# Banded attention and two feed-forward layers on one core: four weight pieces' joins one step later, the second load of v ahead of keys and queries

## The chip, the cores and the metric

One core of a Trainium2 chip runs the whole program. The time is device microseconds of one execution, the median of several. A core has five engines that run their own queues in order and meet at semaphores: TensorE (PE in the profile; its weight loads PEld), VectorE (DVE), ScalarE (ACT), GpSimd (POOL) and SyncE (SP), which issues all the DMA transfers of this kernel. The granted clock of TensorE has two levels, 1.2 GHz (0.5) and 2.4 GHz (1.0).

## The reference

Attention with a local band and block summaries, then two feed-forward layers. Shapes: q, k, v are 2 x 8 x 768 x 64; the first layer is 512 to 2048 to 512, the second 512 to 1024 to 512, on 1536 tokens.

```
k_sum = k.reshape(B, H, nb, 32, D).max(axis=3)
v_sum = v.reshape(B, H, nb, 32, D).mean(axis=3)
scores_l = scale * q @ k.T          # only |i - j| < 16 counts, else -1e9
scores_s = scale * q @ k_sum.T + log(32)
a = softmax(concat(scores_l, scores_s))
x = a @ concat(v, v_sum)            # heads put side by side: 1536 x 512
h = x @ w_in;  x = (h * cos(h)) @ w_out
h = x @ w_in2; solu = h * softmax(h)
out = (layer_norm(solu) * g_ln) @ w_out2
```

The weights come as 64-bit floats.

## The kernel before, in words

The order of the instructions is written out by hand: each engine gets them in the order in which the program names them, and only waits stand between.

The attention takes two heads at a time (a pair n, 0 to 7) and cuts the 768 rows of a pair into 12 tiles of 64 rows; four tiles make a group, so there are three groups to a pair and 24 in all. The loop `for step in range(NGR + LA)` (L663) is a pipeline over groups: n, g = divmod(step, 3). In one step the scores of group step + 1 are made on TensorE (`emit_s`, sps, L561), the maximum of group step on VectorE (`emit_max`, L572) and its subtraction on GpSimd (L576), the exponential of group step - 1 on ScalarE (L581), the sum of step - 2 on VectorE (L585), its normalization on GpSimd (`emit_norm`, L591), the transposes of step - 4 on TensorE (`emit_t`, aps, L598), their copy on ScalarE (`emit_at`, L603), the product with v of step - 5 (`emit_av`, ops, L613) and its copy into X on ScalarE (`emit_x`, L627).

Keys and queries are loaded two pairs or more ahead. In steps with g = 1 (1, 4, 7, 10, 13, 16) VectorE puts the two heads of pair n + 2 side by side (`pair_k`, kg, and `pair_q`, qg, both L426). In the next step, g = 2, TensorE transposes them (`emit_k` L494, `emit_q` L533), and ScalarE copies the queries (`emit_qx` L547). In the step after that, g = 0, VectorE makes the maxima of the key blocks (`emit_ksum` L506) and ScalarE the windows of keys (`emit_kx` L515, `emit_kx_ends` L522, L525 in the next step). The scores of pair n + 2 then need kx.

v is loaded by `load_v` (four DMA issues, L440 and L444, of which two hold the ends); four buffers. `sum_v` (L472) makes its block sums on TensorE at the steps of VSUM_AT, `scale_v` (vm, L480) copies them, `place_vsum` (L487) puts them into v's tile by DMA one step later. The sums of pairs 0 to 6 use the bank that the first product of the feed-forward layer (h, L277) needs at step 19.

A weight piece is 128 x 512 words of 64 bits and goes through these stages, one a step: `bits` at a step of WSTEPS opens it and issues the load of the piece after it (L141, three buffers); in the next step `rebias` (two ScalarE activations, L162 and L163) and `finish` (the join on VectorE, L169); in the step after that `split` (a cast on ScalarE, L186, and a subtraction on GpSimd, L187). The first eight pieces belong to the first layer and go through during the attention. XS are the steps in which a part of X is split in the same way (L246, L247). From step 19 on `fill` puts products of the first layer (h, L277) between the attention's. Behind the attention come the first layer (h L277, y L319) and the second (h L911, L1078), in which the weights of later layers go through the same stages.

Of the kernel before, what the change touches and what calls it, by code (L numbers as in the profile page):

```python
# [34 lines left out]
def fused_kernel(  # L35
# [56 lines left out]

    wide = w_in.dtype == mybir.dt.int64
    LOWEST = -3.0e38
    WSTEPS = (6, 9, 12, 15, 17, 18, 20, 21)
    XS = (7, 10, 13, 16)
    IDLE = (0, 0, 0)
    DVE_X = 19
# [243 lines left out]
    def warm_up(n):  # L342

        if not n:
            return
        idle = idles[0]
        t = ps_h0.tile([P, 512], F32, tag="h", name="idle")
        for _ in range(n):
            nc.tensor.matmul(t, lhsT=idle[:, 0:P], rhs=idle, start=True, stop=True)
# [35 lines left out]
    def attention():  # L385
        st = ExitStack()
        with st:
# [41 lines left out]
            def pair_k(n):  # L429
                k_t[n] = side_by_side(k_t[n], "kg", nc.gpsimd if n == 1 else nc.vector)  # L430

            def pair_q(n):
                q_t[n] = side_by_side(q_t[n], "qg", (nc.gpsimd, nc.scalar)[n] if n < 2 else nc.vector)

            def load_v(n):
                b, hp = divmod(n, NP)
                t = io.tile([P, NT, 2, D], F32, tag="vt", name="vt", bufs=4)
                for j in range(2):
                    o = v[b, 2 * hp + j].offset
                    nc.sync.dma_start(  # L440
                        out=t[0:WIN, 1:NT - 1, j, :],
                        in_=bass.AP(v.tensor, o + (QT - BAND) * D, [[D, WIN], [QT * D, NT - 2], [1, D]]),
                    )
                    nc.sync.dma_start(  # L444
                        out=t[0:WIN, 0:NT:NT - 1, j, :],
                        in_=bass.AP(v.tensor, o, [[D, WIN], [(S - WIN) * D, 2], [1, D]]),
                    )
                v_t[n] = t
# [34 lines left out]
            def place_vsum(n):  # L483
                m = vs_t.pop(n)
                for c in range(2):
                    at = WIN + c * NS // 2
                    nc.sync.dma_start(  # L487
                        out=v_t[n][at:at + NS // 2].rearrange("p t j d -> p t (j d)"),
                        in_=m[D * c:D * c + NS // 2].unsqueeze(1).to_broadcast([NS // 2, NT, 2 * D]))
# [8 lines left out]
            def emit_k(n):  # L498
                qk = ps_qk.tile([P, 2, 2, S // 2], F32, tag="qk", name="qk")
                transposed(k_t.pop(n), qk[:, 0, 0], qk[:, 0, 1])  # L500
                qk_t["k", n] = qk[:, 0]
                qk_t["q", n] = qk[:, 1, 0], qk[:, 1, 1]
# [25 lines left out]
            def emit_q(n):  # L528
                if n < 2:
                    qk_t["q", n] = bank(2, "q0"), bank(3, "q1")  # L530
                t, (a, b) = q_t.pop(n), qk_t["q", n]
                for c in range(NR):
                    nc.tensor.transpose(  # L533
                        (a, b)[c // (NR // 2)][:, (c % (NR // 2)) * P:(c % (NR // 2) + 1) * P],
                        t[:, c].rearrange("p h d -> p (h d)"), ident)
# [17 lines left out]
            def emit_s(G):  # L553
                n, g = divmod(G, GPP)
                qx, kx = kx_t["q", n], kx_t["k", n]
                sps = bank(G % 2, "sps").rearrange("p (i s) -> p i s", i=NG)[:, :, 0:KW]
                for i in range(NG):
                    t = NG * g + i
                    for j in range(2):
                        h = slice(D * j, D * j + D)  # L560
                        nc.tensor.matmul(  # L561
                            sps[h, i, :], lhsT=qx[h, t * QT:(t + 1) * QT], rhs=kx[h, t, :],
                            start=True, stop=True)
                ss_t[G] = sps

            def emit_max(G):
                g = G % GPP
                sm = sm_t[G] = sms[G % NSM]
                sps = ss_t.pop(G)
                mx = sm_p.tile([P, NG], F32, tag="mx", name="mx")  # L570
                for i in range(NG):
                    nc.vector.tensor_tensor_reduce(  # L572
                        out=sm[:, i, 0:KW], in0=sps[:, i, :], in1=mask[:, (NG * g + i > 0) + (NG * g + i == NT - 1), :], scale=1.0, scalar=LOWEST,
                        op0=ALU.add, op1=ALU.max, accum_out=mx[:, i:i + 1])
                sm = sm[:, :, 0:KW]
                nc.gpsimd.tensor_tensor(  # L576
                    out=sm, in0=sm, in1=mx.unsqueeze(2).to_broadcast([P, NG, KW]), op=ALU.subtract)

            def emit_exp(G):
                sm = sm_t[G][:, :, 0:KW]  # L580
                nc.scalar.activation(out=sm, in_=sm, func=AF.Exp)  # L581
# [77 lines left out]
            LX, LN, LT, LA = 1, 2, 4, 5  # L659
            KX_FIRST = (1, 2, 3, 4, 5, 6)  # L660
            VSUM_AT = {1: 0, 4: 1, 8: 2, 10: 3, 12: 4, 15: 5, 18: 6, 20: 7}
            VLOAD_AT = {1: 1, 5: 2, 6: 3, 9: 4, 11: 5, 13: 6, 16: 7}
            for step in range(NGR + LA):  # L663
                n, g = divmod(step, GPP)
                summed = LN <= step < NGR + LN
                ahead = step if step in (1, 2) else n + 1 if g == 0 and 1 < n < NPAIR - 1 else 0

                warm_up(IDLE[g] if step < min(FILL) else 0)
                if step - 1 in VSUM_AT:
                    place_vsum(VSUM_AT[step - 1])  # L670
                if step + 1 < NGR:
                    emit_s(step + 1)
                if step == 0:
                    pair_k(1)
                    emit_max(0)
                    pair_q(1)
                    emit_k(1)
                    emit_q(1)
                if LT <= step < NGR + LT:
                    emit_t(step - LT)  # L680
                if g == 2 and n + 2 < NPAIR:
                    emit_k(n + 2)
                    emit_q(n + 2)
                fill(step)
                if step >= LA:
                    emit_av(step - LA)
                if step in VSUM_AT:
                    sum_v(VSUM_AT[step])

                if g == 1 and n in KX_FIRST:  # L690
                    emit_kx_ends(n + 1)
                if step == NGR:
                    emit_at(step - LT)
                if LX <= step < NGR + LX:
                    emit_exp(step - LX)
                weights.split()
                if 0 < step < NGR and step != 3:
                    emit_max(step)
                if step == 2:
                    emit_max(3)  # L700
                if LT <= step < NGR + LT and step != NGR:
                    emit_at(step - LT)
                if g == 1 and 0 < n < NPAIR - 1 and n not in KX_FIRST:
                    emit_kx_ends(n + 1)
                if ahead and step != 2:
                    emit_ksum(ahead)
                if summed:
                    emit_sum(step - LN)
                if step == 2:
                    emit_ksum(2)  # L710
                if step == NGR + 3:
                    emit_x(step - LA)
                weights.rebias()
                drain(step - NGR, 0)
                weights.finish()
                if summed:
                    emit_norm(step - LN)
                if step >= LA and step != NGR + 3:
                    emit_x(step - LA)
                drain(step - NGR, 1)  # L720
                if ahead:
                    emit_kx(ahead)
                if step == 1:
                    emit_kx_ends(1)
                    emit_qx(1)
                if g == 2 and n + 2 < NPAIR:
                    emit_qx(n + 2)
                if step == 4:
                    weights.load(0)
                if step in WSTEPS:  # L730
                    weights.bits()
                for c in range(KC):
                    if step == XS[c]:
                        xs_of[0, c] = split_x(0, c, xs_a)
                if g == 1 and n + 2 < NPAIR:
                    pair_k(n + 2)
                    pair_q(n + 2)

                if g == 1 and n + 3 < NPAIR:
                    load_k(n + 3)  # L740
                    load_q(n + 3)
                if step in VLOAD_AT:
                    load_v(VLOAD_AT[step])
                if step in VSUM_AT:
                    scale_v(VSUM_AT[step])
# [683 lines left out]
```

## Time and profile before

| what | us |
|---|---|
| median of 3 runs (483.68 to 483.89) | 483.77 |
| the profiled execution | 483.99 |
| its span, first to last instruction | 482.2 |
| its mean granted TensorE clock | 0.995 |

The profile is that of one execution, with times from the start of its span. Something like the first 103 us is the attention; the rest is the two feed-forward layers. A timeline row says start, duration, engine, line, operation, and in brackets how long the engine idled before it and what ended that.

### The profile page before, as it was taken

The numbers are of one execution on the slowest core, as the hardware profiler recorded it, in microseconds if no ns is written. First come the engines' busy times: TensorE is split into PE (matmuls) and PEld (weight loads), VectorE is DVE, ScalarE is ACT, GpSimd is POOL, SyncE is SP. The second block draws the span as 40 slices with busy tenths as digits, with TensorE's granted clock in tenths as the row PEclk, the third lists the DMA queues.
The fourth block names the chain that finished last, engine by engine and source line by source line (L and its number), as shares of the span: only waits on it lengthen the run. The fifth ranks groups of instructions, "written<-read, shape, count | busy, mean of one in ns | idle before, by whom it ended". The sixth has DMA issues, their size and how long they took to land.

```text
span 482.2 us, 8067 instructions
## 1 busy us (share of the span) xinstructions
PE 470.0 (97%) x2899; PEld 385.8 (80%) x2899; DVE 318.1 (66%) x754; ACT 314.2 (65%) x558; POOL 225.0 (47%) x230
## 2 busy tenths in 40 slices
PE   8989889999999999999999999999999999999997
PEld 5867778778888888888888888888888888888876
DVE  4886777673544456465655646574799999988930
ACT  3667788965776865666556655565773348888791
POOL 2676877832422222222222823645204878795450
PEclk9999999999999999999999999999999999999999
DMA  8986972500332223322233112120210021436351
GB/s 213 271 214 171 251 187 75 145 1 1 94 123 88 88 87 109 111 88 87 91 113 102 45 43 88 58 75 1 87 45 1 22 67 43 111 66 112 85 131 67
DMA packets 61304, 46.52 MB, mean 96 GB/s; under 512 B 42704, under 2 KB 53712, under 8 KB 61264
## 3 DMA queue, kind: packets, MB, share of 16 engines
q1 hardware_dynamic: 61264, 46.01, 34.1%
q8 instruction: 23, 0.38, 0.3%
q14 instruction: 17, 0.14, 0.1%
HBM read 36.43 MB, written 3.15 MB: 82 GB/s over the span
## 4 chain that ended last, share of the span: by engine, by line
PE 84%; DVE 5%; ACT 4%; DMA 3%; issue 2%; POOL 1%; SPq 1%; POOLq 0%; ACTq 0%; DVEq 0%
PE y L319 27%; PE h L277 26%; PE h L911 12%; PE h L1078 10%; PE sps L561 2%; PE ops L613 2%; PE vsum L472 1%; PE aps L598 1%; DVE qg L426 1%; DMA vt<-in_v_dram 1%; PE qk L533 1%; DMA qt<-in_q_dram 1%; ACT at L603 1%; ACT kx L515 1%; DMA vt<-vm 1%
## 5 line engine op out<-in xcount | busy, mean ns | idle before, releaser
L277 PE MATMUL h<-xs,w 128*128 128x512 f32 x576 | 140.4, 391 | 0.0
L319 PE MATMUL y<-gs,w 128*128 128x512 f32 x576 | 138.1, 389 | 0.0
L319 PEld LDWEIGHTS y<-gs,w 128*128 128x128 f32 x576 | 108.0, 188 | 22.5
L277 PEld LDWEIGHTS h<-xs,w 128*128 128x128 f32 x576 | 107.4, 188 | 21.9
L187 POOL TENSOR_TENSOR w<-s,w 128x512 fp32r<-128x512 f32 x32 | 42.6, 1332 | 96.9 <-ACT w L186 96.9
L286 ACT ACTIVATE r<-h 128x512 int32<-128x512 f32 x48 | 28.6, 597 | 87.1 <-PE h L277 86.9
L291 DVE SCALAR_TENSOR_TENSOR r<-r,h 128x512 f32<-128x512 int32 x48 | 33.0, 687 | 68.1 <-ACT r L286 67.9
L169 DVE SCALAR_TENSOR_TENSOR s<-raw 128x512 int32<-128x512 int32 x48 | 37.6, 784 | 46.4 <-ACT raw L163 45.2
L1078 PE MATMUL h<-w,ls 128*128 128x512 f32 (+1 forms) x312 | 66.9, 374 | 0.3 <-POOL ls L1055 0.3
L1078 PEld LDWEIGHTS h<-w,ls 128*128 128x128 f32 x312 | 55.3, 188 | 11.3 <-POOL ls L1055 1.1
L911 PE MATMUL h<-w,xo 128*128 128x512 f32 x252 | 58.7, 390 | 0.0
L911 PEld LDWEIGHTS h<-w,xo 128*128 128x128 f32 x252 | 47.2, 188 | 9.7
L296 ACT ACTIVATE r<-r,half_pi 128x512 f32<-128x512 f32 x48 | 34.5, 720 | 5.4 <-DVE r L291 5.3
L307 DVE TENSOR_TENSOR gs<-h,gs 128x512 fp32r<-128x512 f32 x48 | 32.7, 681 | 5.3 <-ACT gs L306 5.3
L301 DVE TENSOR_TENSOR h<-h,r 128x512 f32<-128x512 f32 x48 | 33.1, 689 | 4.2 <-ACT r L296 4.1
L782 POOL TENSOR_TENSOR w<-s,w 128x512 fp32r<-128x512 f32 x14 | 17.9, 1294 | 30.8 <-ACT w L781 30.8
L162 ACT ACTIVATE raw<-raw 128x512 f32<-128x512 f32 x48 | 31.9, 664 | 0.0
L163 ACT ACTIVATE raw<-raw 128x512 int32<-128x512 uint32 x48 | 31.8, 663 | 0.0
L306 ACT ACTIVATE gs<-h 128x512 fp32r<-128x512 f32 x48 | 28.2, 588 | 0.4 <-DVE h L301 0.4
L1048 ACT ACTIVATE s<-turned 128x1024 uint16<-128x1024 uint16 x20 | 26.5, 1365 | 2.3 <-POOL xo L899 1.8
L247 POOL TENSOR_TENSOR xs<-X,xs 128x512 fp32r<-128x512 f32 x10 | 14.0, 1405 | 28.8 <-ACT xs L246 28.8
L591 POOL TENSOR_TENSOR sm<-sm,ss 128x480 f32<-128x480 f32 x24 | 24.7, 1029 | 5.7 <-DVE ss L586 5.2
(105 smaller groups left out, 680.6 us busy)
## 6 DMA issues: line engine op xcount, KB each, us to landing
raw<-in_moe_w_in_dram SPq DMA_DIRECT2D x24, 512.0 KB
raw<-in_moe_w_out_dram SPq DMA_DIRECT2D x24, 512.0 KB
vt<-in_v_dram SPq DMA_DIRECT2D x16, 240.0 KB
kt<-in_k_dram SPq DMA_DIRECT2D x8, 384.0 KB
qt<-in_q_dram SPq DMA_DIRECT2D x8, 384.0 KB
out_dram<-osb SPq DMA_DIRECT2D x11, 256.0 KB
vt<-vm SPq DMA_DIRECT2D x16, 72.0 KB
vt<-in_v_dram SPq DMA_DIRECT2D x16, 48.0 KB
```

Of the source, the lines that this page charges most:

```text
L162: nc.scalar.activation(out=hw, in_=hw, func=AF.Prelu, scale=REBIAS, alpha=NEGATIVE)
L163: nc.scalar.activation(out=lw, in_=lw.bitcast(U32), func=AF.Copy, scale=TOP3)
L169: nc.vector.scalar_tensor_tensor(out=self.f32[i], in0=t[:, :, 1], scalar=3, in1=t[:, :, 0], op0=ALU.logical_shift_left, op1=ALU.bitwise_or)
L187: nc.gpsimd.tensor_tensor(out=w[:, 1, :], in0=f, in1=as32(w[:, 0, :]), op=ALU.subtract)
L277: nc.tensor.matmul(h, lhsT=w[:, a, f * P:(f + 1) * P], rhs=xs_of[tb, c][:, b_, :], start=(m == 0), stop=(m == 3 * KC - 1))
L291: nc.vector.scalar_tensor_tensor(out=r, in0=r.bitcast(I32), scalar=TWO_PI, in1=h_of[step], op0=ALU.mult, op1=ALU.subtract)
L296: nc.scalar.activation(out=r, in_=r, func=AF.Sin, scale=-1.0, bias=half_pi)
L301: nc.vector.tensor_tensor(out=h, in0=h, in1=r, op=ALU.mult)
L307: nc.vector.tensor_tensor(out=gs[:, 1, :], in0=r, in1=as32(gs[:, 0, :]), op=ALU.subtract)
L319: nc.tensor.matmul(y[e], lhsT=w[:, a, e * P:(e + 1) * P], rhs=gs[:, b_, :], start=(f == 0 and i == 0), stop=(f == GF - 1 and i == 2))
L911: nc.tensor.matmul(banks_of[p][BANK[m]], lhsT=x[:, a, s0:s0 + P], rhs=w2_of[m, c][:, b_, :], start=c == j == 0, stop=c == 1 and j == 2)
L1078: nc.tensor.matmul(o, lhsT=ls_of[t][f // 4][:, a, s0:s0 + P], rhs=w[:, b_, cols], start=(f == 0 and i == 0), stop=(f == NF2 - 1 and i == 2))
```

## The change

WSTEPS, the steps at which a weight piece is opened, begins with 7, 10, 13, 16 instead of 6, 9, 12, 15. So the load of the piece behind each of these four, the rebias, the join, the cast and the subtraction of each come one step later: joins in steps 8, 11, 14, 17 (g = 2) instead of 7, 10, 13, 16 (g = 1), where the join stood ahead of `pair_k` and `pair_q` on VectorE. The other four pieces keep their steps; the fourth piece's cast now falls into step 18, with the rebias of the fifth. And the load of v of pair 1 is issued in step 1 ahead of the loads of keys and queries of pair 3 instead of behind them.

```diff
-    WSTEPS = (6, 9, 12, 15, 17, 18, 20, 21)
+    WSTEPS = (7, 10, 13, 16, 17, 18, 20, 21)
     XS = (7, 10, 13, 16)
...
-            VLOAD_AT = {1: 1, 5: 2, 6: 3, 9: 4, 11: 5, 13: 6, 16: 7}
+            VLOAD_AT = {5: 2, 6: 3, 9: 4, 11: 5, 13: 6, 16: 7}
...
                     pair_k(n + 2)
                     pair_q(n + 2)
 
+                if step == 1:
+                    load_v(1)
                 if g == 1 and n + 3 < NPAIR:
                     load_k(n + 3)
                     load_q(n + 3)
```

## Rows read from the trace of the kernel before

**Rows 1.** The page, busy time, share of span and instructions of TensorE.
```profile
PE 470.0 (97%) x2899; PEld 385.8 (80%) x2899; DVE 318.1 (66%) x754; ACT 314.2 (65%) x558; POOL 225.0 (47%) x230
```
**Rows 2.** Waits of TensorE, 9 to 110 us: total, times, longest.
```profile
PE qk L494 <- DVE kg L426: 3.5, 4, 1.5
PE qk L533 <- DVE qg L426: 2.7, 4, 0.7
```
**Rows 3.** Waits of TensorE, 103 to 483 us.
```profile
PE h L1078 <- POOL ls L1055: 0.3, 1, 0.3
```
**Rows 4.** The chain that ended last, 0 to 140 us: start, duration, what.
```profile
30.90 0.54 ACT raw L163
...
32.07 0.55 DVE kg L426
32.63 1.56 DVE qg L426
```
**Rows 5.** TensorE's timeline, attention.
```profile
20.19 1.62 PE L472 MATMUL vsum<-vt,strip 96*64 96x128 f32 x24 [0.33 <-DMA vt<-in_v_dram]
...
22.71 0.65 PE L598 MATMUL aps<-ident,sm 128*120 128x128 f32 x4
...
25.21 1.04 PE L561 MATMUL sps<-kx,qx 64*64 64x120 f32 x16
...
30.51 0.65 PE L598 MATMUL aps<-ident,sm 128*120 128x128 f32 x4
...
38.42 1.04 PE L561 MATMUL sps<-kx,qx 64*64 64x120 f32 x16
...
45.03 0.65 PE L598 MATMUL aps<-ident,sm 128*120 128x128 f32 x4
...
48.87 1.04 PE L561 MATMUL sps<-kx,qx 64*64 64x120 f32 x16
...
50.94 1.48 PE L472 MATMUL vsum<-vt,strip 96*64 96x128 f32 x24
...
55.48 0.65 PE L598 MATMUL aps<-ident,sm 128*120 128x128 f32 x4
...
60.00 1.04 PE L561 MATMUL sps<-kx,qx 64*64 64x120 f32 x16
...
65.64 1.04 PE L561 MATMUL sps<-kx,qx 64*64 64x120 f32 x16
...
75.98 1.64 PE L277 MATMUL h<-xs,w 128*128 128x512 f32 x6
```
**Rows 6.** Busy time of each engine, 34 to 36 us; PEclk is the granted clock.
```profile
core 0: us, PE busy (x) PEld busy (x) DVE busy (x) ACT busy (x) POOL busy (x), PEclk, DMA share, GB/s
34.00:36.00 2.00, 1.77 (x12) 1.44 (x14) 1.97 (x14) 0.00 (x0) 2.00 (x2) 0.50 0.86 203
```
**Rows 7.** VectorE's timeline: a key copy and two joins.
```profile
21.73 0.53 DVE L426 COPY kg<-kt 128x768 f32<-128x768 f32 x1
...
31.47 0.69 DVE L169 SCALAR_TENSOR_TENSOR s<-raw 128x512 int32<-128x512 int32 x1 [1.66 <-ACT raw L163]
...
79.12 1.23 DVE L169 SCALAR_TENSOR_TENSOR s<-raw 128x512 int32<-128x512 int32 x1 [1.82 <-ACT raw L163]
```
**Rows 8.** Waits of VectorE, 22 to 72 us.
```profile
DVE s L169 <- ACT raw L163: 9.7, 4, 3.3
```
**Rows 9.** ScalarE's timeline, steps 15 to 18.
```profile
63.98 0.44 ACT L525 ACTIVATE kx<-ksum 128x288 f32<-128x288 f32 x1
...
71.24 0.38 ACT L627 ACTIVATE X<-ops 128x256 f32<-128x256 f32 x1 [2.05 <-PE ops L613]
...
75.67 0.26 ACT L480 ACTIVATE vm<-vsum 128x128 f32<-128x128 f32 x1
```
**Rows 10.** SP's timeline in step 1.
```profile
10.97 0.40 SPq L408 DMA_DIRECT2D kt<-in_k_dram  x1
...
12.01 0.46 SPq L440 DMA_DIRECT2D vt<-in_v_dram  x1
...
14.87 2.25 SPq L444 DMA_DIRECT2D vt<-in_v_dram  x1
```

## The prediction

> **What bounds the kernel now.** I read the page first: TensorE is busy for 470.0 of 482.2 us [rows 1]. So a gain has to come from the few stretches in which it waits, or from TensorE work itself, and this change removes no TensorE work. I then asked for TensorE's waits in two windows. From 103 us to the end there is a single wait of 0.3 us [rows 3]: behind the attention TensorE has no gap, so whatever the attention gains the end gains, and whatever it loses the end loses. From 9 to 110 us [rows 2] almost all of the waiting is in two lines: 3.5 us in four pieces before the transposes of keys (qk L494 waiting for kg), and 2.7 us in four pieces before those of queries (qk L533 waiting for qg). A third place is the sum of v of step 4: 0.33 us behind a load [rows 5].
>
> The chain of waits says why kg is late [rows 4]: rebias on ScalarE (raw L163, to 31.44), then the join, then kg on VectorE at 32.07, then qg, 1.56 us long. In VectorE's own timeline the join at 31.47 stands behind 1.66 us of idling that ended with ScalarE's raw L163 [rows 7], and from 22 to 72 us there are four such waits, 9.7 us together [rows 8]. These four are the joins of the first four pieces of weights, at steps 7, 10, 13 and 16: all steps in which, right behind the join in VectorE's order, the pairing of keys and queries is queued. TensorE's four pairs of waits stand at the beginning of steps 8, 11, 14 and 17. So a wait for something that nobody needs yet (a weight piece is first multiplied at step 19) holds VectorE, and the pairs that stand behind it hold TensorE.
>
> There is a second price. After the two waits of step 8 the granted clock shows 0.50 from 34 to 36 us [rows 6]: the lower level, 1.2 GHz. TensorE had waited 1.5 and 0.7 us just before. The waits at steps 11, 14 and 17 are not followed by such a fall.
>
> **The change, part by part.** *Joins a step later.* The order given to the chip changes so: in steps 7, 10, 13, 16 VectorE goes from the sums to kg and qg at once; rebias and join come in steps 8, 11, 14, 17, the casts and subtractions in 9, 12, 15, 18. No instruction is added or removed. What TensorE gets back I take from its timeline, from the start of the attention transposes (aps) of a step to the start of the next scores (sps), with the two transpose groups and the outputs (ops) between. Where nothing waited this took 25.21 - 22.71 = 2.50 us (step 5). The others [rows 5]:
> step 8: 38.42 - 30.51 = 7.91, with a sum of v inside it, which at full clock takes 1.48; without waits 2.50 + 1.48 = 3.98, so 3.93 come back, the slow clock's part among them.
> step 11: 48.87 - 45.03 = 3.84, so 1.34.
> step 14: 60.00 - 55.48 = 4.52, so 2.02.
> step 17 shows the same spacing as step 14: 2.02.
> Sum 9.31 us.
>
> *Does something else hold TensorE then?* VectorE: taking the wait of 1.66 and the join of 0.69 away, kg in step 7 begins at 32.07 - 2.35 = 29.7 and qg, even at its slow 1.56 [rows 4], ends near 31.9. TensorE is through aps at 30.51 + 0.65 = 31.2, starts on the keys (ready at 30.3) and comes to the queries at 31.9: just met, at worst some tenths lost. Over the four the waits were longer, 9.7 / 4 = 2.4 on the mean [rows 8], so the margin is larger in the later ones. ScalarE: in step 17 it idled 2.05 us before copying X, waiting for TensorE's ops [rows 9]. The rebias (two instructions like that of 0.54 in [rows 4], 1.08) moves into this gap. TensorE's ops come 2.02 earlier, but ScalarE also loses the rebias (1.08) from step 16 and a cast of the same 128x512 shape (an estimate of 0.54 from the same row) from step 17: 2.05 - 2.02 + 1.08 + 0.54 - 1.08 = 0.6 us of idling is left. So X and the queries' evacuation don't slip: 0, bounds 0 and +1.6 (rival 2). The join itself: VectorE may now wait in steps 8, 11, 14, 17, with the next scores' maximum behind it; TensorE needs that maximum only when the same bank is written again, two score products on. Cost 0. The cast lands in steps 9, 12, 15, in front of the copy of kx: kx was complete at 63.98 + 0.44 = 64.42, the scores that read it began at 65.64 [rows 5, 9], 1.22 of slack against 0.54. Cost 0.
>
> *Step 18* is the one place where I see a cost. The fourth piece's cast now stands in it, ahead of the rebias of the fifth and of the copy vm. That copy ended at 75.67 + 0.26 = 75.93 and frees the bank into which the first h product is written at 75.98 [rows 5, 9]: no slack. 0.54 more on ScalarE is 0 to +0.5, as far as ScalarE has no idling to take it up; I take +0.4.
>
> *Loads of weights.* The raw pieces 1 to 4 are issued a step later, behind a load of v or ahead of one; no bytes are added. Their rebias is a step later too. Cost 0.
>
> *v's second load sooner.* SP issues k(3) at 10.97, q(3), then v(1) from 12.01, its last of four pieces at 14.87 [rows 10]. v(1) moves up 1.04 us; k(3) and q(3) move down by the 5.1 us of issue that v(1) takes (12.01 to about 17.1). v's sum waited 0.33 us for the last piece [rows 5], so the landing, 1.04 earlier, removes that: -0.3. In exchange: the last piece of v landed 5.3 us after its issue began (14.87 to 20.19). By that row k(3), issued at 16.1, lands at 21.4 and q(3), at 16.6, at 21.9; VectorE takes k(3) at 21.73 [rows 7] and q(3) some 0.5 later. Just in time: cost 0, bounds 0 and, if nothing overlaps, +5.1.
>
> *Sum.* 483.99 (the profiled execution: span 482.2 and 1.8 around it) - 9.31 - 0.3 + 0.4 = 474.8. The median of the runs shown is 0.2 lower than this execution, so the forecast is 474.6. All costs at zero and the full 9.31 give 474.1 in the median; small waits behind step 23 may shift by a few tenths, so 473.7 is my lower end.
>
> **One rule against the change.** Beside an idle GpSimd the join took 0.69 us; one that ran beside GpSimd's normalization took 1.23 [rows 7]. In its new place GpSimd has a subtraction and a normalization in hand. The Trainium skill, "SBUF — State Buffer", section "SBUF: two separate sides", says that VectorE instructions with two SBUF inputs and GpSimd instructions exclude one another for a whole instruction. The two rows agree with it in direction. By that rule each of the four joins would cost more; the sum above counts none of it, since VectorE isn't what TensorE waits for.
>
> **The rivals.**
> 1. The longer join reaches TensorE: 4 x (1.23 - 0.69) = 2.2 us given back, 476.8. For: [rows 7]; against: the slack of two score products.
> 2. Rebias in front of X and qx delays the keys' copies: 1.08 + 0.54 = 1.62 added against 1.22 of slack, 0.4 a cycle, four times 1.6 us: 476.2. For: ScalarE has only 0.6 us a cycle left by my working; against: the idling that the row shows.
> 3. k(3) and q(3) late: up to 5.1 us at step 5, so up to 479.7; against: the landing worked out above.
> 4. The pairs wait all the same, for something that the join's wait covered, the exponentials or the loads of keys and queries: 483.8, no change. For: nothing in the waits; against: kg starts right behind the join, and SP issued those loads a whole cycle ahead.
> 5. Slower: the join's wait is recreated at steps 8, 11, 14, 17, and the maximum behind it comes too late for its bank. If the 9.7 us of VectorE's waits [rows 8] go to TensorE in full, with the 2.2 of rival 1: 474.6 + 9.7 + 2.2 = 486.5. It decides only when VectorE falls behind by more than 2.3 us a cycle (9.3 / 4) over the slack of two score products; against: the rebias fits into idling of ScalarE.
>
> **How the numbers follow.** Full removal 0.70 (474.6); rival 1 0.08; rival 2 0.07; rival 3 0.05; rival 4 0.05; rival 5 0.05. The range 473.7 to 477.5 takes in the first three cases, 0.85. A change under 0.2% (1 us) is about what a measurement can't tell from none. Faster: the first four cases, 0.90; same 0.05; slower 0.05.
>
> **What would show it.** In the changed kernel's profile: no wait of qk L494 for kg and at most a few tenths for qg; aps to sps near 2.5 us in steps 11, 14 and 17; the granted clock at 1.00 through the stretch that was 0.50; the joins' waits on VectorE still there, behind qg; v's sum of step 4 without a wait for its load; the first h product waiting some tenths for vm. I am wrong if TensorE shows new waits on kx, on X or on the scores' bank at steps 9 to 12, or if VectorE's kg waits for a load at step 4 or 10, where the DMA queue has the least time in hand.

## The result and the profile after

The changed kernel takes 475.27 us (median of 4, 474.64 to 476.79) against 483.73 before (median of 4): a ratio of 0.9832, 95% interval 0.9807 to 0.9857. The profiled execution took 474.64, 9.35 less than the one before; its span is 472.9.

TensorE's waits in the attention, 9 to 103 us of the changed kernel (total, times, longest), answer to [rows 2]:

```profile
PE h L277 <- ACT vm L480: 0.6, 1, 0.6
PE sps L561 <- ACT kx L525: 0.6, 2, 0.3
PE aps L598 <- POOL sm L591: 0.3, 1, 0.3
PE aps L598 <- ACT at L603: 0.2, 1, 0.2
PE qk L533 <- DVE qg L426: 0.2, 1, 0.2
```

The 3.5 us before the keys are gone, of the 2.7 before the queries 0.2 is left, and a new line leads: the first h product waits for vm. TensorE's timeline of the changed kernel, against [rows 5]:

```profile
19.23 1.53 PE L472 MATMUL vsum<-vt,strip 96*64 96x128 f32 x24
20.97 1.04 PE L561 MATMUL sps<-kx,qx 64*64 64x120 f32 x16 [0.21 <-ACT kx L525]
...
29.82 0.65 PE L598 MATMUL aps<-ident,sm 128*120 128x128 f32 x4
...
31.29 0.88 PE L533 MATMUL qk<-ident,qg 128*128 128x128 f32 x6 [0.17 <-DVE qg L426]
...
34.02 1.04 PE L561 MATMUL sps<-kx,qx 64*64 64x120 f32 x16
...
40.63 0.65 PE L598 MATMUL aps<-ident,sm 128*120 128x128 f32 x4
...
43.14 1.04 PE L561 MATMUL sps<-kx,qx 64*64 64x120 f32 x16
...
49.75 0.65 PE L598 MATMUL aps<-ident,sm 128*120 128x128 f32 x4
...
52.26 1.04 PE L561 MATMUL sps<-kx,qx 64*64 64x120 f32 x16
...
58.87 0.65 PE L598 MATMUL aps<-ident,sm 128*120 128x128 f32 x4
...
61.38 1.04 PE L561 MATMUL sps<-kx,qx 64*64 64x120 f32 x16
...
65.83 0.65 PE L598 MATMUL aps<-ident,sm 128*120 128x128 f32 x4
67.11 1.65 PE L277 MATMUL h<-xs,w 128*128 128x512 f32 x6 [0.64 <-ACT vm L480]
```

The spacing from the start of aps to that of the next scores is 34.02 - 29.82 = 4.20 in step 8 (7.91 before), 2.51 in step 11 (3.84), and 2.51 in steps 14 and 17 (4.52). From the aps of step 19 to the first h it is 1.28, before 0.41 (75.98 - 75.57). Step 8 lies at 30 to 34 us now; its granted clock, against [rows 6]:

```profile
30.00:34.00 4.00, 3.83 (x56) 3.28 (x55) 3.97 (x13) 3.64 (x7) 4.00 (x4) 1.00 1.02 283
```

VectorE's timeline around steps 7, 8 and 17, against [rows 7]:

```profile
29.02 0.95 DVE L426 COPY kg<-kt 128x768 f32<-128x768 f32 x1
29.90 1.34 DVE L426 COPY qg<-qt 128x768 f32<-128x768 f32 x1
...
32.74 1.14 DVE L169 SCALAR_TENSOR_TENSOR s<-raw 128x512 int32<-128x512 int32 x1
...
62.06 1.39 DVE L169 SCALAR_TENSOR_TENSOR s<-raw 128x512 int32<-128x512 int32 x1 [1.55 <-ACT raw L163]
```

The pair comes first, the join behind it, still waiting for ScalarE where it has to; that wait now holds nothing that TensorE needs at once.

### The profile page after: what moved, and what is told of

Same layout as the page of the kernel before. It is cut to its first block, busy times and chain, and to the rows that moved or that the text cites. A ratio compares the mean times of both kernels' runs of the same rounds, so it can differ in the third digit from the quotient of the medians.

```text
span 472.9 us, 8062 instructions
## 1 busy us (share of the span) xinstructions
PE 466.6 (99%) x2899; PEld 384.8 (81%) x2899; DVE 318.9 (67%) x754; ACT 314.3 (66%) x558; POOL 227.7 (48%) x230
## 4 chain that ended last, share of the span: by engine, by line
PE 93%; DVE 2%; ACT 2%; DMA 1%; SPq 1%; POOL 0%; issue 0%; DVEq 0%; ACTq 0%
PE y L319 28%; PE h L277 27%; PE h L1080 14%; PE h L913 12%; PE sps L561 3%; PE ops L613 2%; PE aps L598 2%; PE vsum L472 2%; PE qk L494 1%; PE idle L349 1%; ACT kx L515 1%; DMA raw<-in_moe_w_out_dram 1%; PE qk L533 1%; DVE ksum L506 1%; DVE sm L572 1%; SPq L444 1%
## 5 line engine op out<-in xcount | busy, mean ns | idle before, releaser
L187 POOL TENSOR_TENSOR w<-s,w 128x512 fp32r<-128x512 f32 x32 | 41.3, 1292 | 97.1 <-ACT w L186 97.0
L169 DVE SCALAR_TENSOR_TENSOR s<-raw 128x512 int32<-128x512 int32 x48 | 39.0, 812 | 39.2 <-ACT raw L163 37.9
L784 POOL TENSOR_TENSOR w<-s,w 128x512 fp32r<-128x512 f32 x14 | 17.9, 1295 | 30.8 <-ACT w L783 30.8
L591 POOL TENSOR_TENSOR sm<-sm,ss 128x480 f32<-128x480 f32 x24 | 27.7, 1157 | 2.2 <-DVE ss L586 1.7
L576 POOL TENSOR_TENSOR sm<-sm,mx 128x480 f32<-128x480 f32 x24 | 25.0, 1044 | 6.8 <-DVE mx L572 6.8
```

What stands on the lines that cost most here:

```text
L169: nc.vector.scalar_tensor_tensor(out=self.f32[i], in0=t[:, :, 1], scalar=3, in1=t[:, :, 0], op0=ALU.logical_shift_left, op1=ALU.bitwise_or)
L187: nc.gpsimd.tensor_tensor(out=w[:, 1, :], in0=f, in1=as32(w[:, 0, :]), op=ALU.subtract)
```

## The experiments

Theory 1 is the prediction's: a join that waits for ScalarE stood ahead of the pairing in VectorE's queue, and that was nearly the whole. Theory 2: the gain comes from ScalarE, whose rebias left crowded steps for a gap. Theory 3: the load of v gives much of it. Each kernel's ratio is to the kernel before in the same rounds.

**One part alone.** `e1_joins_only`: the new WSTEPS with the old VLOAD_AT.

> The four joins a step later, the load of v where it was. Theory 1 (a join that waits for ScalarE stands ahead of the pairing in VectorE's queue, and this is nearly the whole): TensorE's waits for kg and qg at steps 8, 11, 14 and 17 are gone, the spacings from aps to sps are 2.5 us, v's sum of step 4 waits 0.3 us as before; about 8.2 us less than before, 475.5. Theory 3 (the load of v, which shifts all that follows it, gives a large part): clearly above 477.

Measured 476.46, ratio 0.9844 (0.9828 to 0.9860). TensorE's spacings are those of the changed kernel (4.21, 2.50, 2.51, 2.51); v's sum of step 4 waited 0.68 us in this profile, not 0.3. `e2_vload_only`: the old WSTEPS, the load of v sooner.

> Only the second load of v sooner, the joins as before. Theory 1: the wait of v's sum, 0.3 us, goes and TensorE's four pairs of waits stay: 483.4, within 0.4 of before. Theory 3: several us less than before, below 481.

Measured 482.82, ratio 0.998 (0.9953 to 1.0008). The joins are the change; theory 3 falls. The median lies 1.2 below that of the kernel before, where at most 0.4 was expected. The profile of e2 also shows something about the clock. TensorE waits in step 8 as before the change, to a hundredth, and its clock does not fall (33 to 37 us):

```profile
33.00:37.00 4.00, 3.19 (x48) 2.79 (x50) 3.97 (x20) 1.95 (x5) 4.00 (x4) 1.00 0.78 174
```

```profile
33.13 0.87 PE L494 MATMUL qk<-ident,kg 128*128 128x128 f32 x6 [1.52 <-DVE kg L426]
34.68 0.88 PE L533 MATMUL qk<-ident,qg 128*128 128x128 f32 x6 [0.67 <-DVE qg L426]
```

(The first is a row of busy times as above, the second two rows of TensorE's timeline.) Its spacing in step 8 is 6.45 us, not 7.91. So 1.46 of the 7.91 were the lower clock, and not every execution pays them. Of e2's 11 executions one has a mean granted clock below 0.999, of the 15 of the kernel before beside it 10; whether the sooner load of v has a part in that, no run isolates.

**Order or place.** `e3_join_behind`: the joins stay in their old steps, behind kg and qg; the rebias and the load of v stay.

```diff
-                weights.finish()
+                behind = step in (7, 10, 13, 16)
+                if not behind:
+                    weights.finish()
...
                     pair_q(n + 2)
+                if behind:
+                    weights.finish()
```

> Before, with the joins in the same steps 7, 10, 13, 16 but behind kg and qg on VectorE; the rebias stays in these steps on ScalarE, the load of v stays. Theory 1: only the order on VectorE matters, so the waits for kg and qg go, and the cast of the fourth piece stays in step 17, so the first h product doesn't wait for vm: 474.5 to 475. Theory 2 (the gain comes from ScalarE, whose rebias left the crowded steps for a gap in the next one): the gain is missing or less than half, 480 to 483.7.

Measured 476.02, ratio 0.9851 (0.9827 to 0.9874). The spacings are those of the changed kernel (4.21, then 2.51 three times), with the rebias where it always was: theory 2 falls, the order on VectorE is enough. One part of the expectation failed, and the time is a microsecond over its figure. The cast of the fourth piece is in step 17 here, and h waits for vm all the same, longer (TensorE's timeline, then ScalarE's):

```profile
67.55 1.65 PE L277 MATMUL h<-xs,w 128*128 128x512 f32 x6 [1.03 <-ACT vm L480]
```

```profile
63.94 0.60 ACT L581 ACTIVATE sm<-sm 128x480 f32<-128x480 f32 x1 [1.10 <-POOL sm L576]
```

The exponential of step 18 waited 1.10 us for GpSimd's subtraction, which stood behind the subtractions of a part of X and of the fourth piece (60.45 to 62.97). From there to vm at 67.20 ScalarE has no gap. So a full GpSimd makes vm late also without the cast in step 18.

**One piece, three pieces.** `e11_first_piece_only`: WSTEPS (7, 9, 12, 15, ...) in the kernel before.

> Before, with the first weight piece alone opened a step later (7, 9, 12, 15). Theory 1: TensorE's waits of step 8 go and with them the stretch at the lower clock, 3.7 to 3.9 us; the waits of steps 11, 14, 17 stay: 479.9. If the fall of the clock came from something else than the waits just before it, the lower level stays and only the waits themselves, about 2.3 us, come back: 481.4.

Median 481.32 (479.92 to 482.69), ratio 0.9949 (0.9922 to 0.9975). Its profiled execution, the fastest, has the spacings 4.21, 3.97, 4.51, 4.51: step 8's waits went and the other three stayed, as theory 1 has it. The median lies 1.4 above my figure; no profile shows where. It is close to the figure for the other case, a lower clock that stays, but that is not what happened: seven of the eight executions have a mean granted clock of 1.000. `e12_last_three_only`: WSTEPS (6, 10, 13, 16, ...).

> Before, with the second to fourth piece a step later (6, 10, 13, 16) and the first as it was. Theory 1, the four being independent: the waits of steps 11, 14, 17 go, 5.4 us, less 0.9 us at the first h product; the waits of step 8 and the lower clock behind them stay: 479.2. If the waits are tied to each other (one removed comes back at the next): less than 3 us under before, above 480.7.

Measured 478.81, ratio 0.9900 (0.9871 to 0.9929), spacings 6.47, then 2.51, 2.51 and 2.50, h 0.9 later behind aps. In the profiles the four waits are independent: from the first scores to the first y product e11 took 3.72 us less than before and e12 5.70, of which 1.44 was the clock, counted in both; together 7.98, against 8.30 with all four gone.

**The new wait.** `e4_vm_first`: in step 18 the copy vm stands ahead of the copy of kx.

```diff
+                if step == 18:
+                    scale_v(6)
                 if ahead:
                     emit_kx(ahead)
...
-                if step in VSUM_AT:
+                if step in VSUM_AT and step != 18:
                     scale_v(VSUM_AT[step])
```

> The changed kernel, with the copy vm of step 18 ahead of the copy of kx on ScalarE. If the wait of 0.64 us of the first h product is for that copy, behind a cast that is new in this step: the wait goes or falls under 0.1 us, the start of h stands 0.4 us behind that of aps as before, and the time is 0.8 us under the changed kernel's of the same rounds, 474.5. If something else would hold h anyway: no difference, 475.3.

Measured 475.04, ratio 0.9822 (0.9805 to 0.9839). h no longer waits and starts 0.41 behind aps; from the first scores to the first y product this execution took 84.81 us, the changed kernel's 85.51. In the medians 0.7 us is not told apart. `e6_cast_at_19`: the fourth piece's cast and subtraction held back to step 19.

```diff
+                held = []
+                if step == 18:
+                    held, weights.ready = weights.ready, []
                 weights.split()
...
                 weights.finish()
+                weights.ready = held + weights.ready
```

> The changed kernel, with the fourth piece's cast and subtraction held back from step 18 to step 19; vm stays behind the copy of kx. If the cast makes vm late, as the prediction has it: the first h product no longer waits, 0.9 us under the changed kernel, 474.4. If ScalarE comes late into step 18 in any case (it copied X 0.5 us behind TensorE's outputs in step 17): about 0.5 of the 0.87 us come back and 0.3 to 0.4 us of waiting is left, 474.8.

Measured 476.41, ratio 0.9857 (0.9839 to 0.9875). From aps to h 0.70 us instead of 1.28: 0.58, about what the cast takes, came back there and 0.3 stayed, since ScalarE comes late into step 18 in any case. But aps of a later step then waited 1.0 us for `at`, so the total did not fall and lies above both figures.

**The changed kernel again.** `e5_changed_again`: no edit.

> The changed kernel itself, to stand beside the next three in the same rounds and to see how far its executions lie apart: 475.3, between 474.6 and 476.8. Where two executions differ, theory 1 expects the difference ahead of step 1 (the landing of the first load of queries) and none between steps 5 and 18.

Measured 475.80 (475.10 to 477.16), ratio 0.9844. The profiled execution was the slowest, and against the expectation it differs at step 18. ScalarE's timeline, then TensorE's row of h, then SP's:

```profile
64.59 0.57 ACT L603 ACTIVATE at<-aps 120x512 f32<-120x512 f32 x1
66.42 0.67 ACT L162 ACTIVATE raw<-raw 128x512 f32<-128x512 f32 x1 [1.26 <-DMA raw<-in_moe_w_out_dram]
...
68.71 0.27 ACT L480 ACTIVATE vm<-vsum 128x128 f32<-128x128 f32 x1
```

```profile
69.04 1.66 PE L277 MATMUL h<-xs,w 128*128 128x512 f32 x6 [2.36 <-ACT vm L480]
```

```profile
55.34 2.81 SPq L444 DMA_DIRECT2D vt<-in_v_dram  x1
58.65 1.66 SPq L487 DMA_DIRECT2D vt<-vm  x2
60.42 0.46 SPq L141 DMA_DIRECT2D raw<-in_moe_w_out_dram  x1
```

The fifth piece's load moved with WSTEPS from step 15 to step 16, two steps ahead of its rebias. In the first profile it was issued at 58.58 and nothing waited for it. Here issues of v took longer, it left at 60.42, and the rebias, with vm behind it, came 1.26 us late. `e9_load_sooner` puts `weights.load(4)` back to step 15:

> The changed kernel, with the load of the fifth weight piece issued at step 15 again, as before, instead of step 16. In one profile of the changed kernel ScalarE's rebias in step 18 waited 1.3 us for that load and the first h product then 2.4 us for vm; in another it waited for nothing and h 0.6 us. If that load is what spreads the executions: no wait of raw L162 for a load, h waits 0.6 us in the profile, the median is 0.3 to 0.8 us under the changed kernel's (475.3 and 475.8 in two sets), 475.0. If the spread comes from the first loads alone: no difference.

Median 476.09 (475.03 to 476.16), ratio 0.9832 (0.9799 to 0.9864): in its profile no wait for the load and 0.6 us for vm, but a median no lower than the changed kernel's. So the late load is shown in one execution; no run shows that it spreads the executions in general. `e10_load_and_vm` has both edits:

> The changed kernel with both: the fifth piece's load at step 15 and vm ahead of the copy of kx in step 18. If both costs are what the profiles show: no wait of the first h product, and the lowest time of all, 474.2 to 474.8. If one of them was covered by the other: as with the copy of vm alone, 475.0.

Measured 474.75 (474.10 to 475.51), ratio 0.9813 (0.9780 to 0.9845), from the first scores to the first y product 84.84: the lowest median of all, with an interval that overlaps the changed kernel's.

**How much room is left.** `e7_double_join`: the first four joins done twice, into the same place.

```diff
                 self.join_one(self.queue[-1])
+                if self.queue[-1] < 4:
+                    self.join_one(self.queue[-1])
```

> The changed kernel with each of the first four joins done twice, into the same place, so VectorE has 0.7 to 1.2 us more in steps 8, 11, 14 and 17, and GpSimd runs beside it. Theory 1 (VectorE has the slack of two score products there): TensorE gets no new wait on steps 9 to 17 except tenths, 475.3 to 475.9. Rival 1 (the longer join reaches TensorE): 2.8 to 4.8 us more, 478 to 480.

Measured 479.80, ratio 0.9925 (0.9909 to 0.9941): my expectation failed and rival 1's held. Busy times of 50 to 61 us in e7, and the changed kernel's of 49 to 58 and 58 to 67 (columns as in [rows 6]: TensorE, its loads, VectorE, ScalarE, GpSimd):

```profile
50.00:61.00 11.00, 9.74 (x145) 7.78 (x144) 10.86 (x38) 8.86 (x21) 9.56 (x9) 1.00 0.73 190
```

```profile
49.00:58.00 9.00, 9.00 (x146) 7.71 (x144) 8.52 (x36) 8.39 (x18) 8.71 (x8) 1.00 0.90 231
58.00:67.00 9.00, 8.48 (x128) 7.18 (x128) 7.38 (x25) 8.36 (x18) 9.00 (x9) 1.00 0.92 256
```

Two joins took 2.5 to 2.7 us together, VectorE has no idling left, and the cycle of three steps grows to about 10.7 us (kg at 50.84 and 61.58). In the changed kernel it is 9.1 (aps of steps 14 and 17 at 49.75 and 58.87). Of the two stretches above VectorE fills 0.95 and 0.82, ScalarE 0.93 of both, GpSimd 0.97 and all.

`e8_step_earlier`: WSTEPS (5, 8, 11, 14, ...), joins at g = 0.

> The changed kernel with the first four pieces opened at 5, 8, 11, 14: joins in steps 6, 9, 12, 15 (g = 0), also clear of the pairing, but with the rebias ahead of the copy of kx on ScalarE. Theory 1: TensorE's waits for kg and qg stay away and the fourth piece's cast is done before step 18; the rebias of 1.1 us ahead of kx meets about 0.6 us of slack before the scores that read kx, so up to 0.5 us of new waiting in each of three or four cycles: 475.5 to 477. Rival 2 in full (ScalarE's order is what limits): 478 or more. If place doesn't matter at all beside the pairing: 474.4.

Measured 482.06, ratio 0.9964 (0.9941 to 0.9987), outside all that I had written except rival 2's "or more", and the wait is not rival 2's. VectorE's timeline of step 6, then TensorE's row:

```profile
28.65 1.18 DVE L169 SCALAR_TENSOR_TENSOR s<-raw 128x512 int32<-128x512 int32 x1 [0.50 <-ACT raw L163]
29.76 0.27 DVE L572 CUSTOM_DVE_ANT_0 sm<-sps,mask 128x120 f32<-128x120 f32 x1
```

```profile
30.79 1.04 PE L561 MATMUL sps<-kx,qx 64*64 64x120 f32 x16 [1.17 <-DVE mx L572]
```

The next scores' maximum stands behind the join and the scores wait for its bank: the mechanism of rival 5, at g = 0. It shows twice, 2.3 us in all, of the 6.3 by which the stretch from the first scores to the first y product is longer than in the changed kernel (91.78 against 85.51). Besides, aps waited 1.1 us for `at`, h 0.4 more for vm, and from 54 to 56 us the granted clock is 0.56. The clock is not what made the median: the executions with a mean clock of 1.000 took 481.67 to 482.25 too. The rest is not worked out.

## Why the prediction was right, and where its terms were off

- *The cause* held: e1 and e3 show that moving the join behind the pairing, in the same step or the next, removes TensorE's waits, and e2 that the load of v alone gives no clear difference.
- *Steps 11, 14, 17*: 1.34, 2.02 and 2.02 forecast, 1.33, 2.01 and 2.01 measured.
- *Step 8*: 3.93 forecast, 3.71 measured; 0.17 is the wait for qg, the "just met" of the working. But 1.46 of it was the lower clock, which the profiled executions of e2 and e12 did not pay with the same waits. So it is a price that some executions pay, and the prediction took it, from one profile, as paid by all. Of the 41 executions of the kernel before that ran beside the experiments, 18 have a mean granted clock of 0.996 or less (median 484.4 us) and 23 one of 0.999 or 1.000 (483.0): 1.4 us apart. Of the 41 of the changed kernel, e1, e3, e4, e5, e6, e7, e9 and e10, where the waits of steps 8, 11, 14 and 17 are gone or small, none lies below 0.999; of e8's and e11's 8 each, with waits elsewhere, 2 and 1 do. That the low stretch lies at step 8 in the executions without a profile is not shown.
- *ScalarE's 0.6 us of idling in step 17* was wrong. ScalarE's timeline of the changed kernel:

```profile
59.80 0.60 ACT L581 ACTIVATE sm<-sm 128x480 f32<-128x480 f32 x1 [0.64 <-POOL sm L576]
...
61.92 0.37 ACT L627 ACTIVATE X<-ops 128x256 f32<-128x256 f32 x1
...
63.48 0.63 ACT L186 ACTIVATE w<-s 128x512 fp32r<-128x512 f32 x1
...
66.79 0.27 ACT L480 ACTIVATE vm<-vsum 128x128 f32<-128x128 f32 x1
```

The exponential waited 0.64 us for GpSimd, and X was copied at 61.92, 0.5 behind the end of TensorE's ops (60.76 + 0.69). The working counted ScalarE's own work and not its wait for GpSimd, which by then had none to spare: its normalization and subtraction there (57.20, 58.47) took 1.31 and 1.30 us beside the copies kg and qg. Beside a join one took 1.43 to 1.45, beside neither 0.98 or 0.99.
- *Step 18*: +0.4 forecast, 0.87 measured (1.28 - 0.41), 2.6 in the execution of e5 (69.04 - 66.03 - 0.41). The cast is two thirds of the 0.87 (e6), the late ScalarE the rest. But with the cast back in step 17 (e3) h started 1.68 behind aps, later still. The working asked only whether ScalarE has idling to take up the cast; a wait for GpSimd ahead of it cost more.
- *Loads of weights*, taken at nothing, cost 1.3 us in one of two profiles of this kernel. The bytes were the same, but the load of the fifth piece had lost a step of lead.
- *The load of v*: 0.3 forecast. From the first scores to those of step 5 (9.31 to 21.74, 8.76 to 20.97) it was 0.22: the wait for the load went and 0.21 came back at kx. In e3, with the old order, there was no such wait at all (21.00 - 8.79 = 12.21, as in the changed kernel). Over all profiles this stretch took 12.20 to 12.78 with the old order (five) and 12.20 to 12.22 with the new (seven of nine; e2 12.56, e6 12.68). So this part is worth 0 to 0.6.
- *Rival 1, the longer join.* The joins did get longer (1.39 us in step 17, 0.69 alone), as the Trainium skill, "SBUF — State Buffer", section "SBUF: two separate sides", would have it, and so did kg (0.73 to 1.21, with 0.55 before). It stayed off TensorE's path but for the 0.17 us at qg, yet the working's reason, "the slack of two score products", was too generous: e7 shows that a second join, 1.2 to 1.4 us a cycle, is too much.

The sum in place: from the first scores to the first y product 93.81 (9.31 to 103.12) before, 85.51 (8.76 to 94.27) after, 8.30 less, against 9.2 forecast. The other 1.05 us between the two profiled executions lie outside the change: 0.55 before the first scores, where the first load of queries lands, 0.45 behind the first y product and 0.05 outside the spans. Over all the profiles of this study the first scores began between 8.66 and 9.77 and the stretch behind the first y took 378.6 or 379.0 to 379.2. That the profiled execution came out 0.2 from its forecast of 474.8 is thus luck: the 0.9 by which the terms were too favourable (0.5 at step 18, 0.2 at step 8) is offset by 1.05 from outside the change. The median fell by 8.46, 0.7 less than forecast. The price of the clock, counted in full and paid by fewer than half of the executions of the kernel before, may be part of that; this is not shown.

## What to carry to other kernels

When an in-order engine waits, look at what is queued behind the waiting instruction before asking for a faster supplier: putting the one piece of work that is not due soon behind the pieces that are gave 8 us without an instruction less (e3). When the order moves, follow the loads that move with it: a load whose bytes and queue are the same can still lose its lead. And ask of a freed stretch which engine is full there now; here, from 49 to 58 us, all four are busy for over 0.9 of the time, so the same kind of move has little left to give.

## What the runs showed of the hardware

- The same two waits of TensorE, 1.5 and 0.7 us at the same place, were followed by the lower clock (0.50) in one kernel's profile and by 1.00 in two others'. In 18 of 41 executions of that first kernel the mean clock is 0.996 or less. What decides it, no run here tells.
- VectorE's key copy, 128x768, took 0.53 to 0.56 us in every profiled instance of the kernel before, and 0.73 to 1.21 in steps 7, 10, 13 and 16 of the changed kernel, where GpSimd had an operation running at its start. That operation kept its length; the one behind it took 1.30 or 1.31 instead of 0.98 or 0.99. In all four the copy ended 0.41 to 0.42 us behind the end of GpSimd's operation, and the joins of steps 8, 11, 14 and 17 ended 0.55 to 0.57 behind it. That fits VectorE waiting for what was left of that operation, so the price hangs on when the copy or the join starts. One copy and one join of the changed kernel, each with the GpSimd operation that was running:

```profile
37.68 0.99 POOL L591 TENSOR_TENSOR sm<-sm,ss 128x480 f32<-128x480 f32 x1
37.87 1.21 DVE L426 COPY kg<-kt 128x768 f32<-128x768 f32 x1
...
61.91 0.98 POOL L576 TENSOR_TENSOR sm<-sm,mx 128x480 f32<-128x480 f32 x1
62.06 1.39 DVE L169 SCALAR_TENSOR_TENSOR s<-raw 128x512 int32<-128x512 int32 x1 [1.55 <-ACT raw L163]
```

- The issue of v's last piece ahead of the fifth weight piece held SP for 2.00 us in one execution and 2.81 in another of the same kernel: an issue's length differs between executions.
